# POOL's weight differences in the experts' arms: two operations of 512 columns in place of one of 1,024

## The chip, the cores and the metric

One core of a Trainium2 chip runs the whole kernel as one program. The metric is the device time of that program in microseconds, the median of the runs shown. The engines are named as the profile names them: PE multiplies matrices (PEld is its weight load), DVE is the vector engine, ACT the scalar engine, POOL is GpSimd, and SP's queue issues most of the DMAs.

## The reference

The program computes attention with a few sink keys and a sliding window, and feeds its output to a layer of eight experts in which a token may stay with the expert of the token before it.

```python
scores = scale * np.matmul(q, k.transpose(0, 1, 3, 2))      # B, H, S, D = 4, 8, 768, 64
keep = is_sink | in_window                                  # 4 sinks, window of 128
...                                                         # softmax over the kept keys
x = attn_out.transpose(0, 2, 1, 3).reshape(B, S, H * D)     # 3,072 tokens of 512
e = fresh_e if s == 0 or local_gate[b, s] < 0.5 else prev_e # one expert of 8 for each token
h = np.maximum(x[b, s] @ w1[e], 0.0)                        # 512 -> 1,024
out[b, s] = p[e] * (h @ w2[e])                              # 1,024 -> 512, times the gate
```

## The kernel before

The first part, up to about 255 us of the span, is attention, routing and the scatter of the tokens into the DRAM tensor `xs`, sorted by expert. The change does not touch it.

The second part walks over the eight experts. PE multiplies in a float32 form with shortened mantissa, so each operand is split into a high part (a rounding copy) and a low part (the difference of the original and the high part). A product is the sum of high by high, low by high and high by low. Both the tokens and the weights are split this way on the core.

**Weights.** The weights of an expert come in eight chunks of 128 x 1,024 float32, four of `w1` and four of `w2`. A chunk is loaded by SP into one of seven staging buffers (`raw`, `raw_w`), by `w_load`. `w_split` then queues its split: two copies of 512 columns by ACT (L1031, the high part `h`), and the difference (L1032, the low part `l`). Chunks alternate between two ways, `ENG = (("act", "pool"), ("act", "dve"))`: for every second chunk the difference is POOL's, for the others DVE's. High and low parts of a half of an expert's weights fill one of three buffers, `w_a`, `w_b` and `w_c`. For a `w2` chunk the staging buffer's next load, `w_load(i + AHEAD)`, is queued behind the split.

**Arms.** How many tokens an expert has is known only at run time. For each expert the program holds 25 arms, one for each count of 32-token blocks, and all engines jump to the one that is needed. In an arm, `ffn1` makes eight tiles of the hidden layer (`h`, in PSUM, three buffers; L1126, or L1115 where the group has at most seven blocks), ACT writes their high part to `hq` (L1137) and DVE their low part (L1102). `ffn2` and `second` make the second product (L1175). In between PE transposes the next expert's tokens (`xp`, L427, two PSUM buffers). For each of these ACT takes the high part (L430) and DVE the low part (L433).

**Order.** PE, ACT, DVE and SP run an arm's instructions in the order in which the code emits them. An `Agenda` holds pieces of work with a due time of the writer's own clock and emits them between the tiles of PE; `w_agenda` puts the splits there, with `lag` between the pieces of a chunk. POOL's queue holds the differences and the indirect DMAs of the results (L1157).

Of the kernel before, what the change touches and what calls it, by code (L numbers as in the profile page):

```python
# [23 lines left out]
E, DM, FF = 8, 512, 1024  # L24
# [46 lines left out]
def kernel(ctx, tc, qkd, vn, vs, w1, w2, nw, c_misc, c_ident, c_idw, c_small,  # L71
# [400 lines left out]
    def w1_of(e):  # L472
        return [t.rearrange("p (k f) -> p k f", k=KC) for t in half(e, 0)]

    def w2_of(e):
        return [lambda f, n=1, t=t: t[:, f * DM:(f + n) * DM] for t in half(e, 1)]
# [7 lines left out]
    halves = [slice(0, HP), slice(HP, FF)]  # L484
# [527 lines left out]
    def w_load(i, behind=None):  # L1012
        e, c = divmod(i, NCH)
        if e >= E:
            return
        t = raw_t[i % AHEAD]
        if c < KC:
            d = nc.sync.dma_start(t, w1[e, c * P:(c + 1) * P, :])
            if behind is not None:
                tc.add_manual_dep(d.ins, behind.ins.name, mybir.DependencyInfo(  # L1020
                    mybir.DependencyClass.Sync, mybir.DependencyReason.DATA), reason="behind the jumps")
        else:
            w2_load(t, e, c - KC)

    def w_split(ag, i, t, eng, lag=0.9):
        e, c = divmod(i, NCH)
        raw = raw_t[i % AHEAD] if e else second_raw[c - KC]
        h, l = [t[:, c, :] for t in w1_of(e)] if c < KC else [t(2 * (c - KC), 2) for t in w2_of(e)]
        hi = nc.scalar.copy if eng[0] == "act" else nc.vector.tensor_copy
        lo = (nc.gpsimd if eng[1] == "pool" else nc.vector).tensor_tensor  # L1030
        todo = [lambda s=s: hi(h[:, s], raw[:, s]) for s in halves]  # L1031
        todo += [lambda s=s: lo(out=l[:, s], in0=raw[:, s], in1=h.bitcast(F32)[:, s], op=ALU.subtract)  # L1032
                 for s in ([slice(0, FF)] if eng[1] == "pool" else halves)]
        for k, f in enumerate(todo):
            ag.add(t + lag * k, f)
        if e and c >= KC:
            ag.add(t + lag * (len(todo) - 1), lambda: w_load(i + AHEAD))

    def w_agenda(ag, e, c0, c1, t0, step, eng):
        for c in range(c0, c1):  # L1040
            w_split(ag, e * NCH + c, t0 + step * (c - c0), eng[c % len(eng)], min(0.9, 0.5 * step))
# [405 lines left out]
```

## Time and profile before

| | |
|---|---|
| time before, median of three runs | 572.18 us (572.16 to 575.89) |
| the profiled execution | 568.84 us, span 567.1 us |
| PE busy | 524.3 us, 92% of the span |
| DVE busy | 337.2 us, 59% |
| ACT busy | 283.3 us, 50% |
| POOL busy | 227.2 us, 40% |
| POOL's differences of weights in the arms (L1032) | 28 of 128x1024, 69.2 us in all (25.1 + 24.7 + 19.4) |

The span is the time from the first to the last instruction of the program in one profiled execution; that execution's own time holds 1.74 us beside it. A row of a timeline gives the start in us from the span's start, the duration in us, engine, line, operation, output and inputs, shape and count; what stands in brackets is the idle time of that engine just before, and what ended it. "issue" in that place means that the profile shows nothing that was waited for.

### The profile page before, as it was taken

The page shows a single profiled execution, that of the slowest core. Times are in us where ns is not written, and L with a number is a line of the kernel's source. Part 1 is how long each engine was busy: PE and PEld are TensorE (multiplying, and loading weights), DVE is VectorE, ACT ScalarE, POOL GpSimd, SP SyncE. Part 2 cuts the span into 40 slices and gives each one's busy share as a digit, 9 for nine tenths or more (in the row PEclk, how much of TensorE's full clock was granted, in tenths as well). Part 3 has the DMA queues.
Part 4 walks back from the last instruction along what each step waited for, and adds up shares of the span by engine and source line. Part 5 has one row for each costly group of instructions (what it writes and reads, how often), then busy time and mean ns, then how long its engine had stood idle before and what let it go on. Part 6 is the DMA issues. An engine that isn't in the chain of part 4 may idle for free. (4 is left out here: it accounts for less than half of the span.)

```text
span 567.1 us, 11850 instructions
## 1 busy us (share of the span) xinstructions
PE 524.3 (92%) x3947; PEld 446.9 (79%) x3947; DVE 337.2 (59%) x1270; ACT 283.3 (50%) x854; POOL 227.2 (40%) x191
## 2 busy tenths in 40 slices
PE   6699989979997989998999999899999999999994
PEld 3498878768886868778989788879877688889893
DVE  4677868787877878655348184753464947253321
ACT  3588867776877785253344181624332544124120
POOL 3963616383466064425350161544403544104101
PEclk8599979998998999999999999999999999999998
DMA  8634313162426025366760274737514765111000
GB/s 296 228 140 180 114 66 123 59 230 82 157 94 225 2 106 194 119 192 206 222 227 30 79 271 143 279 111 270 166 41 153 237 200 222 56 45 37 20 24 35
DMA packets 30474, 80.54 MB, mean 142 GB/s; under 512 B 3646, under 2 KB 5310, under 8 KB 30272
## 3 DMA queue, kind: packets, MB, share of 16 engines
q1 hardware_dynamic: 25520, 65.41, 33.9%
q0 software_dynamic: 4176, 12.64, 5.9%
q14 instruction: 147, 1.20, 0.7%
q8 instruction: 55, 0.90, 0.7%
q10 hardware_dynamic: 576, 0.39, 0.2%
HBM read 63.41 MB, written 16.06 MB: 140 GB/s over the span
## 5 line engine op out<-in xcount | busy, mean ns | idle before, releaser
L621 ACT ACTIVATE pef<-smf,biasf 128x264 f32<-128x264 f32 (+2 forms) x192 | 93.6, 489 | 43.2 <-DVE biasf L618 43.0
L1137 ACT ACTIVATE hq<-h 128x32 fp32r<-128x32 f32 (+4 forms) x112 | 32.0, 316 | 141.7 <-PE h L1126 92.5
L1102 DVE SCALAR_TENSOR_TENSOR hq<-h,hq 128x32 fp32r<-128x32 f32 (+4 forms) x112 | 34.4, 332 | 67.2 <-ACT hq L1137 65.6
L618 DVE CUSTOM_DVE_ANT_0 smf<-sf,mask 128x264 f32<-128x264 f32 (+2 forms) x192 | 66.6, 402 | 10.2 <-PE sf L606 9.8
L1175 PE MATMUL late<-w_a,hq 128*128 128x512 f32 (+2 forms) x288 | 70.4, 398 | 1.2 <-issue 1.2
L1175 PEld LDWEIGHTS late<-w_a,hq 128*128 128x128 f32 (+2 forms) x288 | 50.8, 179 | 16.1 <-issue 2.1
L1157 POOL DMA_INDIRECT out_dram<-ot_d,oi_d x18 | 18.9, 1051 | 92.3 <-DVE ot_d L1156 72.6
L636 PE MATMUL tpf<-ident,pef 128*128 128x128 f32 x352 | 53.4, 294 | 0.3 <-ACT ptf L643 0.2
L643 ACT COPY ptf<-tpf 128x512 f32<-128x512 f32 (+1 forms) x96 | 51.0, 531 | 1.7 <-PE tpf L636 1.6
L672 PE MATMUL avf<-ptf,v 128*64 128x128 f32 x704 | 49.8, 282 | 0.0
L636 PEld LDWEIGHTS tpf<-ident,pef 128*128 128x128 f32 x352 | 40.3, 148 | 8.2 <-ACT ptf L643 1.4
L1175 PE MATMUL late<-w_b,hq 128*128 128x512 f32 (+1 forms) x168 | 40.5, 397 | 1.8 <-issue 1.8
L672 PEld LDWEIGHTS avf<-ptf,v 128*64 128x64 f32 x704 | 38.0, 138 | 4.9 <-issue 0.3
L1175 PEld LDWEIGHTS late<-w_b,hq 128*128 128x128 f32 (+1 forms) x168 | 30.7, 184 | 9.8 <-ACT x_a L430 2.0
L578 DVE TENSOR_TENSOR xb<-bkf,rsf 128x256 f32<-128x256 f32 x48 | 20.3, 423 | 30.3 <-ACT ptsf L653 28.6
L1032 POOL TENSOR_TENSOR w_c<-raw,w_c 128x1024 fp32r<-128x1024 f32 x10 | 25.1, 2515 | 31.1 <-ACT w_c L1031 26.0
L606 PE MATMUL sf<-w_a 64*128 64x264 f32 (+2 forms) x288 | 28.6, 333 | 9.3 <-POOL w_a L136 6.2
L621 ACT ACTIVATION_READ_ACCUMULATOR pef<-smf,biasf 128x1 f32 x192 | 36.3, 189 | 0.0
L1126 PEld LDWEIGHTS h<-x_a,w_c 128*128 128x128 f32 x288 | 34.4, 188 | 0.5 <-issue 0.3
L1032 POOL TENSOR_TENSOR w_a<-raw,w_a 128x1024 fp32r<-128x1024 f32 x10 | 24.7, 2465 | 25.0 <-ACT w_a L1031 19.4
L1126 PE MATMUL h<-x_a,w_c 128*128 128x256 f32 x288 | 34.6, 281 | 0.0
L606 PEld LDWEIGHTS sf<-w_a 64*128 64x128 f32 x288 | 22.4, 216 | 14.9 <-POOL w_a L136 7.0
(225 smaller groups left out, 1089.6 us busy)
## 6 DMA issues: line engine op xcount, KB each, us to landing
raw<-in_dram SPq DMA_DIRECT2D x53, 512.0 KB, 5.3
raw<-in_dram SPq DMA_DIRECT2D x14, 800.0 KB, 6.0
xr_0n<-xs SPq DMA_DIRECT2D x21, 258.0 KB, 4.5
v<-in_dram SPq DMA_DIRECT2D x7, 768.0 KB, 4.6
raw_w<-in_dram SPq DMA_DIRECT2D x7, 512.0 KB, 4.9
raw<-in_dram SPq DMA_DIRECT2D x10, 256.0 KB, 4.6
xs<-zrow SPq DMA_DIRECT2D x9, 258.0 KB, 5.2
xr_0r<-xs SPq DMA_DIRECT2D x8, 258.0 KB, 3.0
```

Source lines behind the costliest of these rows:

```text
L578: nc.vector.tensor_tensor(out=xb[:, i, g * HG * D:(g + 1) * HG * D].rearrange("p (r t d) -> p r t d", r=NPR, t=2), in0=av[:, :, 0:P].rearr ...
L606: u["mm"] = nc.tensor.matmul(sps[:, t, :w], qx[ROWS[t], i * P:(i + 1) * P], kx[ROWS[t], off:off + w], start=m == 0, stop=m == 2)
L618: u["dve"] = nc.vector.tensor_tensor_reduce(out=sm[:, :w], in0=sps[:, t, :w], in1=mk, scale=-0.125, scalar=BIG, op0=ALU.add, op1=ALU.min, ...
L621: nc.scalar.activation(pe[:, h, :w], sm[:, :w], AF.Exp, bias=bias[:, t:t + 1], scale=-1.0, accum_out=z[:, h, 0:1])
L636: nc.tensor.transpose(tp[:, t, k, :], pe[:, 2 * c + t, o:o + P], ident)
L643: nc.scalar.copy(pt[:, :, 0:nt, :], tp[:, :, 0:nt, :])
L672: nc.tensor.matmul(avt[ROWS[t], pr, :], prep["v"][:, j, 2 * pr + t, :], x["pt"][:, t, k, :], start=i < 2 and pr == 0 and k == 0, stop=pr = ...
L1032: todo += [lambda s=s: lo(out=l[:, s], in0=raw[:, s], in1=h.bitcast(F32)[:, s], op=ALU.subtract) for s in ([slice(0, FF)] if eng[1] == "po ...
L1102: nc.vector.scalar_tensor_tensor(out=d[:, :, 1, :], in0=h, scalar=0.0, in1=d.bitcast(F32)[:, :, 0, :], op0=ALU.max, op1=ALU.subtract)
L1126: nc.tensor.matmul(hs, w[:, k, fs], x, start=t == 0, stop=t == len(mm) - 1)
L1137: relu = nc.scalar.activation(d[:, :, 0, :], h, AF.Relu)
L1175: nc.tensor.matmul(o, a, w, start=t == 0, stop=t == len(mm) - 1, skip_group_check=half)
```

## The change

In `w_split`, the difference that POOL makes was one operation over all 1,024 columns of a chunk. It becomes two operations over 512 columns each, one queued `lag` behind the other on the agenda, as DVE's were already. The copies by ACT stay two of 512 columns. Where the chunk is one of `w2`, the piece that emits the staging buffer's next load is due with the last piece of the split, and so one `lag` later on the agenda's clock.

```diff
         lo = (nc.gpsimd if eng[1] == "pool" else nc.vector).tensor_tensor
         todo = [lambda s=s: hi(h[:, s], raw[:, s]) for s in halves]
         todo += [lambda s=s: lo(out=l[:, s], in0=raw[:, s], in1=h.bitcast(F32)[:, s], op=ALU.subtract)
-                 for s in ([slice(0, FF)] if eng[1] == "pool" else halves)]
+                 for s in halves]
         for k, f in enumerate(todo):
             ag.add(t + lag * k, f)
         if e and c >= KC:
```

The sequences of PE, DVE, ACT and SP stay the same, instruction by instruction. What differs is POOL's sequence, and what some instructions of the other engines wait for.

POOL, in the arm that expert 3 takes in the profiled execution (11 blocks, 352 tokens), with what each instruction waits for. `w_b` takes the `w2` of this expert, `w_c` the `w1` of the next, and `ot` is a tile of results. Before:

```order
L1032 TENSOR_TENSOR w_b<-raw,w_b 128x1024 [waits DMAHW4_49,DMAHW1_49,DMAHW6_49,PE_49,DMAHW7_49,Activation_49,Pool_49]
L1032 TENSOR_TENSOR w_b<-raw,w_b 128x1024 [waits DMAHW0_49,DMAHW1_49,PE_49,DMAHW3_49,Activation_49,Pool_49]
L1157 DMA out_dram<-ot_10_d_40466,oi_10_d_40467 3072x512 [waits DMASW6_49,DVE_49]
L1032 TENSOR_TENSOR w_c<-raw,w_c 128x1024 [waits PE_49,DMAHW0_49,Activation_49,Pool_49]
L1032 TENSOR_TENSOR w_c<-raw,w_c 128x1024 [waits PE_49,DMAHW2_49,Activation_49,Pool_49]
L1157 DMA out_dram<-ot_10_0_2_40639,oi_10_0_2_40640 3072x512 [waits DMASW7_49,DVE_49]
```

The same place of the changed kernel:

```order
L1032 TENSOR_TENSOR w_b<-raw,w_b 128x512 [waits DMAHW4_49,DMAHW6_49,DMAHW1_49,DMAHW7_49,PE_49,Activation_49]
L1032 TENSOR_TENSOR w_b<-raw,w_b 128x512 [waits PE_49,Activation_49]
L1032 TENSOR_TENSOR w_b<-raw,w_b 128x512 [waits DMAHW1_49,DMAHW3_49,DMAHW0_49,Activation_49]
L1032 TENSOR_TENSOR w_b<-raw,w_b 128x512 [waits PE_49,Activation_49]
L1157 DMA out_dram<-ot_10_d_40734,oi_10_d_40735 3072x512 [waits DMASW6_49,DVE_49]
L1032 TENSOR_TENSOR w_c<-raw,w_c 128x512 [waits DMAHW0_49,PE_49,Activation_49]
L1032 TENSOR_TENSOR w_c<-raw,w_c 128x512 [waits PE_49,Activation_49]
L1032 TENSOR_TENSOR w_c<-raw,w_c 128x512 [waits DMAHW2_49,PE_49,Activation_49]
L1032 TENSOR_TENSOR w_c<-raw,w_c 128x512 [waits PE_49,Activation_49]
L1157 DMA out_dram<-ot_10_0_2_40910,oi_10_0_2_40911 3072x512 [waits DMASW7_49,DVE_49]
```

Four operations became eight, each with a wait of its own for ACT's copy of its half. Their waits for POOL's own earlier work are gone, and the indirect DMAs of the results keep their places between the chunks.

PE, in the same arm, at the first matrix products of `ffn2` (`o` is the tile of the last 96 tokens). Before:

```order
L1175 MATMUL o_10_0_2_40609<-w_b,hq 96x512 [waits Activation_49]
L1175 MATMUL o_10_0_2_40609<-w_b,hq 96x512
L1175 MATMUL o_10_0_2_40609<-w_b,hq 96x512 [waits Pool_49]
L1175 MATMUL o_10_0_2_40609<-w_b,hq 96x512 [waits Activation_49]
L1175 MATMUL o_10_0_2_40609<-w_b,hq 96x512 x2
L1175 MATMUL o_10_0_2_40609<-w_b,hq 96x512 [waits Activation_49]
```

And in the changed kernel:

```order
L1175 MATMUL o_10_0_2_40879<-w_b,hq 96x512 [waits Activation_49]
L1175 MATMUL o_10_0_2_40879<-w_b,hq 96x512
L1175 MATMUL o_10_0_2_40879<-w_b,hq 96x512 [waits Pool_49]
L1175 MATMUL o_10_0_2_40879<-w_b,hq 96x512 [waits Activation_49]
L1175 MATMUL o_10_0_2_40879<-w_b,hq 96x512
L1175 MATMUL o_10_0_2_40879<-w_b,hq 96x512 [waits Pool_49]
L1175 MATMUL o_10_0_2_40879<-w_b,hq 96x512 [waits Activation_49]
```

The product that reads the second half of a low part now has a wait for POOL of its own, where the one wait, three products earlier, had stood for the whole chunk. No instruction was added on PE for it.

## The prediction, made before the changed kernel ran

> **What bounds the kernel now.** I read the page's shares first, then the stretches of the second part, then PE's gaps there.
>
> ```profile
> PE 524.3 (92%) x3947; PEld 446.9 (79%) x3947; DVE 337.2 (59%) x1270; ACT 283.3 (50%) x854; POOL 227.2 (40%) x191
> 335.00:365.00 30.00, 28.31 (x154) 24.12 (x153) 19.03 (x41) 13.53 (x33) 12.93 (x7) 1.00 0.56 182
> 425.00:455.00 30.00, 28.17 (x151) 21.27 (x149) 20.12 (x49) 12.40 (x35) 12.26 (x6) 1.00 0.55 185
> sum 312.00, PE 297.16 PEld 256.48 DVE 151.97 ACT 110.50 POOL 100.65; mean PE 27.01 PEld 23.32 DVE 13.82 ACT 10.04 POOL 9.15
> ```
>
> PE sets the time. The last row sums eleven stretches from 255 us to the end: PE is busy for 297.16 of 312 us. Two of the stretches (columns: PE, PEld, DVE, ACT, POOL, granted clock, DMA share, GB/s) are those where most is lost, under 2 us each, and the granted clock there is 1.00. POOL is busy for a third of the time. So POOL's work matters only through those for whom it makes PE wait. The rows of PE's timeline that have a gap of over 0.2 us ahead of them:
>
> ```profile
> 268.78 5.85 PE L1175 MATMUL late<-w_b,hq 128*128 128x512 f32 x24 [1.78 <-issue]
> 316.15 5.85 PE L1175 MATMUL late<-w_a,hq 128*128 128x512 f32 x24 [0.96 <-issue]
> 363.18 0.63 PE L427 MATMUL xp_0n<-ident,xr_0n 128*128 128x128 f32 x4 [1.69 <-issue]
> 425.91 5.85 PE L1175 MATMUL late<-w_a,hq 128*128 128x512 f32 x24 [0.24 <-issue]
> 439.64 1.28 PE L1115 MATMUL h<-x_a,w_b 128*128 128x320 f32 x8 [0.29 <-DVE hq L1102]
> 449.42 5.83 PE L1175 MATMUL late<-w_c,hq 128*128 128x512 f32 x24 [1.01 <-issue]
> 456.50 16.89 PE L1126 MATMUL h<-x_b,w_a 128*128 128x384 f32 x96 [1.25 <-issue]
> ```
>
> They come to 7.22 us. Five of them (5.24 us) stand at the edge of an arm, ahead of the first products behind a jump or of a new arm, where the profile names no engine. The other two (1.98 us) lie inside arms, and both are DVE's, as the next rows show. That is the whole stake: 0.35% of 568.84.
>
> ```profile
> 357.27 0.62 ACT L1031 CAST w_b<-raw 128x512 fp32r<-128x512 f32 x1
> 358.26 0.64 ACT L1031 CAST w_b<-raw 128x512 fp32r<-128x512 f32 x1
> 359.03 2.40 POOL L1032 TENSOR_TENSOR w_b<-raw,w_b 128x1024 fp32r<-128x1024 f32 x1 [1.85 <-ACT w_b L1031]
> 357.93 0.68 DVE L1032 TENSOR_TENSOR w_b<-raw,w_b 128x512 fp32r<-128x512 f32 x1
> 359.37 2.61 DVE L1032 TENSOR_TENSOR w_b<-raw,w_b 128x512 fp32r<-128x512 f32 x1
> 361.90 0.57 DVE L1102 SCALAR_TENSOR_TENSOR hq<-h,hq 128x96 fp32r<-128x96 f32 x2
> 362.40 0.68 DVE L433 TENSOR_TENSOR x_b<-xp_0n,x_b 128x512 fp32r<-128x512 f32 x1
> ```
>
> The same DVE operation takes 0.68 us at 357.93 and 2.61 us at 359.37. The second runs beside POOL's difference and ends at 361.98, 0.55 us behind POOL's end at 361.43: DVE stood still until POOL was through. Then come L1102 and L433, which ends at 363.08 and gives free the PSUM buffer that PE's transposes at 363.18 need. PE's gap of 1.69 us is DVE's stall of 1.93, handed on.
>
> **The change, part by part.** First what an operation costs POOL. The rows are of two views by line (ns: least, median, greatest); the last is another loop of the kernel with the new shape.
>
> ```profile
> L1032 POOL TENSOR_TENSOR w_c<-raw,w_c x10: 2362/2398/2922, 262.3 to 476.6; 128x1024 fp32r<-128x1024 f32 x10
> L1032 POOL TENSOR_TENSOR w_a<-raw,w_a x10: 2387/2406/2826, 277.9 to 521.9; 128x1024 fp32r<-128x1024 f32 x10
> L1032 POOL TENSOR_TENSOR w_b<-raw,w_b x8: 2387/2403/2544, 287.2 to 464.7; 128x1024 fp32r<-128x1024 f32 x8
> L508 POOL TENSOR_TENSOR w_a<-raw,w_a x8: 1270/1281/1328, 201.2 to 217.9; 128x512 fp32r<-128x512 f32 x8
> ```
>
> 28 operations of 2.40 us become 56 of 1.28: two halves take 2.56, so 0.16 us more for a chunk and 28 x 0.16 = 4.5 us more POOL work. On the path this costs nothing, since POOL stands idle for two thirds of these stretches; without that cover it would be 4.5 us, 0.8%. And a chunk is done earlier. The first half need not wait for ACT's second copy: at 359.03 ACT had ended its copies at 357.89 and 358.90, about 1 us apart, so the second half could start as before and end 2.40 - 1.28 = 1.1 us sooner. Where the copies follow each other directly (0.62 apart), the end moves by 0.62 + 2.40 - 2.56 = 0.46 us. Who gains from that?
>
> ```profile
>   DVE oi_d L1151: 1.6, 1
>   PEld late L1175: 0.2, 1
> SPq L494 <- POOL w_c L1032: 7.6, 4, 2.1
> SPq L494 <- POOL w_a L1032: 7.2, 4, 2.3
> SPq L494 <- POOL w_b L1032: 1.4, 1, 1.4
> ```
>
> The first two rows are all that waited for L1032 on engines, with their total; PEld's 0.2 us was under running products. SP's loads of staging buffers (L494) wait for POOL nine times, 16.2 us in all, and would start 0.5 to 1.1 us sooner. As the load's place in SP's sequence is the same, the later due time in `w_split` costs nothing; and since PE nowhere waits for weights, an earlier load is worth nothing either. The added waits of PE and ACT for POOL sit on instructions that are there already. The new one on PE stands three products (some 1.2 us) behind the old, with the weights done well before: I take zero. For a ceiling I use the 0.05 us of a separate wait on another queue of this trace, times three such waits for each of eight experts: 1.2 us.
>
> ```profile
> L1126 PEldq EVENT_SEMAPHORE  x16: 51/51/51, 274.0 to 513.2; - x16
> ```
>
> Now the stalls. What DVE does when POOL has two operations in a row is shown at two other places.
>
> ```profile
> 17.88 1.87 POOL L136 TENSOR_TENSOR hq<-raw,hq 128x800 fp32r<-128x800 f32 x1
> 19.71 1.79 POOL L136 TENSOR_TENSOR w_a<-raw,w_a 128x544 fp32r<-128x544 f32 x1
> 18.13 2.17 DVE L136 TENSOR_TENSOR w_a<-raw,w_a 128x512 fp32r<-128x512 f32 x1 [1.40 <-ACT w_a L131]
> 202.44 1.33 POOL L508 TENSOR_TENSOR w_a<-raw,w_a 128x512 fp32r<-128x512 f32 x1
> 202.57 1.27 DVE L346 TENSOR_TENSOR exf<-exf,ohs 128x48 f32<-128x48 f32 x1
> ```
>
> At 18.13 DVE waited for POOL's first operation and ended at 20.30, 0.55 us behind that one's end and long before the end of POOL's second, which was queued right behind. So DVE, once waiting, goes first, and a stall ends with the half that runs. At 202.57 it is the new shape that blocks: DVE's operation ends 0.07 us behind POOL's.
>
> Worked out at 359: the first half is ready at about 358.0, waits for DVE's operation of 357.93 to 358.61, and runs to 359.9. DVE's next, at 359.37, waits till 359.9 and ends at 360.6 in place of 361.98. That is 1.4 us earlier, and PE's gap shrinks by about that: **1.3 us**, bounded by zero and 1.69. At 439.64 the cause is this pair:
>
> ```profile
> 435.86 2.38 POOL L1032 TENSOR_TENSOR w_c<-raw,w_c 128x1024 fp32r<-128x1024 f32 x1 [7.71 <-ACT w_c L1031]
> 437.40 1.39 DVE L1032 TENSOR_TENSOR w_c<-raw,w_c 128x512 fp32r<-128x512 f32 x1
> ```
>
> DVE loses 0.71 us to POOL's end at 438.24. With two halves the first can start near 434.9 and the second ends near 437.5, so the stall goes and with it **0.3 us** of PE's gap. The sum: 568.84 - 1.3 - 0.3 = 567.2 us for the profiled execution, 0.3% less. That execution was 3.3 us under the median of the runs shown, so for the median it is 572.18 - 1.6 = **570.6 us**. A measurement of this kernel tells about 1% from no change, and this is a third of that.
>
> The Trainium skill weighs on the step that was least certain. "SBUF — State Buffer", section "Who interferes with whom", says that DVE instructions with two SBUF inputs contend with POOL's reads, that whoever issues first gets the shared ports for its whole instruction, and that the other blocks fully. The rows at 359.37 and 18.13 agree. Read against the change, the rule would let POOL's second half go first whenever it is issued ahead of DVE's operation; the second rival prices that from rows. By the rule read so the sum would be 571.4 us, by the row at 18.13 it is 570.6.
>
> **The rivals.** *Nothing is left of the gain (0.20).* POOL's halves fall on DVE at other moments, what is won at 363 is lost elsewhere, and the time is 572.2.
>
> ```profile
> L1032 DVE TENSOR_TENSOR w_a<-raw,w_a 128x512 fp32r<-128x512 f32 x14 | 12.9, 963 | 0.0
> L1032 DVE TENSOR_TENSOR w_b<-raw,w_b 128x512 fp32r<-128x512 f32 x12 | 11.6, 977 | 0.0
> L1032 DVE TENSOR_TENSOR w_c<-raw,w_c 128x512 fp32r<-128x512 f32 x12 | 8.6, 740 | 0.0
> ```
>
> For it: against 0.68 us for an undisturbed one, these three groups (mean ns behind the busy time) lose some 8 us, and PE lost only 2 us, so most stalls fall where PE has slack, and it is chance which do not. Against it: halves stall DVE for about half as long, wherever they fall.
>
> *POOL keeps the ports through both halves (0.12).* DVE at 359.37 then waits until 361.2 at best (358.6 + 2.56) and the gain there is 0.75 us; if it arrives early in the first half, it waits 0.16 us longer than now. Time: 571.4 to 572.4. The row at 18.13 speaks against it.
>
> *New stalls in the arms, slower (0.10).* POOL's first halves start up to 1 us sooner, and so DVE meets POOL where it did not. The place that hurts is an L1032 of DVE queued ahead of L433, the low part of the next tokens: PE has two PSUM buffers for the transposes, and waits when both are held. The price is that of the place at 363, at most 1.69 us, or 1.3 with a half. Two such new places outweigh the 1.6 us; four give 572.18 - 1.6 + 5.2 = 575.8, and six would be over 1%.
>
> *The edges of the arms shift (0.05).* The five gaps ahead of jumps, 0.24 to 1.78 us, have no releaser and may hang on which transfers run then. Loads that start sooner could clear them (-5.2, 565.4) or add as much at the edges that have none (575.8 to 580).
>
> **How the numbers follow.** The forecast, a gain of 1 to 2.3 us, has 0.53; its own range is 569.9 to 571.2. The range to the other cases: below, the two gaps and one or two edge gaps gone (4 us, 568.0); above, two new stalls of 1.3 us on top of the time before (574.8, so 575.0), which takes in the ceiling of 1.2 us for the waits. Over 1% faster needs all the edge gaps and DVE's to clear together (565.4): 0.02. Over 1% slower needs six new stalls or most of the edges: 0.03.
>
> **What would show it.** 56 operations of L1032 on POOL at 1.28 us; no DVE operation beside them above about 2 us; the gap ahead of L427 in expert 3's arm under 0.5 us; the product counts and the edge gaps as now. I am wrong if DVE's longest L1032 still takes 2.6 us, if PE gets gaps inside other arms, or if the edge gaps change by more than the two that I count.

## The result, and the profile after

The changed kernel takes 577.87 us (median of 22 runs, 573.33 to 580.0) against 571.03 us for the kernel before in 22 runs beside it. The ratio is **1.0114, with a 95% interval of 1.0095 to 1.0133**: about 6.5 us slower. The forecast was 570.6 us with a range of 568.0 to 575.0. So the forecast was wrong in sign, and the time lies outside the range.

First the page's shares, and the second part of the span (window: length; then PE, PEld, DVE, ACT and POOL busy, granted clock, DMA share, GB/s).

```profile
PE 529.6 (92%) x3947; PEld 449.9 (78%) x3947; DVE 347.4 (60%) x1270; ACT 283.7 (49%) x854; POOL 235.7 (41%) x219
255.00:577.00 322.00, 302.09 (x1746) 259.39 (x1744) 162.76 (x403) 110.75 (x283) 109.92 (x87) 0.98 0.41 136
```

The same window of the kernel before:

```profile
255.00:567.10 312.10, 297.16 (x1740) 256.48 (x1738) 151.97 (x403) 110.50 (x283) 100.65 (x58) 0.99 0.41 140
```

The page's instruction counts agree but for POOL's 28 more. In this window PE's idle time grew from 14.94 to 19.91 us, by 4.97. That is the part of the loss that lies in PE's waits. DVE is busy 10.8 us longer for the same 403 operations, so it stands still for longer. PE's busy time grew as well, over the whole span by 5.3 us at the same 3,947 products, and here the granted clock is the place to look:

```profile
255.00:275.00 20.00, 18.41 (x115) 16.24 (x114) 8.65 (x34) 5.69 (x16) 9.83 (x9) 0.91 0.55 176
425.00:455.00 30.00, 26.70 (x146) 20.09 (x145) 18.06 (x59) 11.81 (x37) 9.03 (x8) 0.94 0.53 170
```

The kernel before had 1.00 in both stretches. Two later runs with the same new gaps (the changed kernel repeated, and the one with `w2` alone split) had 1.00 in both as well, so I take these two dips for the luck of this one execution. They may be why the two profiled executions lie 9.9 us apart and the medians only 6.8; no run shows that.

Now the rows of PE's timeline in the arms with a gap of over 0.2 us ahead of them, as quoted for the kernel before:

```profile
269.63 7.38 PE L1175 MATMUL late<-w_b,hq 128*128 128x512 f32 x24 [1.59 <-ACT x_a L430]
287.96 1.68 PE L1126 MATMUL h<-x_a,w_c 128*128 128x256 f32 x12 [0.79 <-DVE hq L1102]
319.72 5.86 PE L1175 MATMUL late<-w_a,hq 128*128 128x512 f32 x24 [1.03 <-issue]
337.73 0.63 PE L427 MATMUL xp_0n<-ident,xr_0n 128*128 128x128 f32 x4 [1.79 <-issue]
391.76 9.78 PE L1126 MATMUL h<-x_b,w_c 128*128 128x256 f32 x84 [1.63 <-issue]
402.54 1.68 PE L1126 MATMUL h<-x_b,w_c 128*128 128x256 f32 x12 [1.00 <-DVE hq L1102]
432.47 5.85 PE L1175 MATMUL late<-w_a,hq 128*128 128x512 f32 x24 [0.32 <-issue]
439.07 7.01 PE L1115 MATMUL h<-x_a,w_b 128*128 128x320 f32 x48 [0.76 <-PE late L1175]
450.09 1.76 PE L1115 MATMUL h<-x_a,w_b 128*128 128x320 f32 x8 [2.09 <-DVE xm L429]
464.98 16.91 PE L1126 MATMUL h<-x_b,w_a 128*128 128x384 f32 x96 [0.46 <-PE late L1175]
533.26 1.69 PE L1126 MATMUL h<-x_a,w_c 128*128 128x256 f32 x12 [0.79 <-DVE hq L1102]
```

The two gaps inside arms that the prediction wanted to shrink (1.98 us) are gone. **Five new ones** stand at other places, at 287.96, 337.73, 402.54, 450.09 and 533.26: 0.79 + 1.79 + 1.00 + 2.09 + 0.79 = 6.46 us. The gaps at the edges of arms come to 5.79 us (5.24 before). So of PE's 4.97 us more of idle time, 4.48 lie inside arms.

What stands behind the gap at 287.96 is read from POOL and DVE in expert 1's arm. POOL first:

```profile
283.43 1.00 POOL L1157 DMA_INDIRECT out_dram<-ot_d,oi_d  x1 [1.06 <-ACT hq L1137]
284.45 2.57 POOL L1032 TENSOR_TENSOR w_a<-raw,w_a 128x512 fp32r<-128x512 f32 x2
```

and DVE, from the later of its two differences on:

```profile
284.37 3.21 DVE L1032 TENSOR_TENSOR w_a<-raw,w_a 128x512 fp32r<-128x512 f32 x1
287.50 0.74 DVE L1102 SCALAR_TENSOR_TENSOR hq<-h,hq 128x256 fp32r<-128x256 f32 x2
```

POOL issues the indirect DMA and then, without a pause, both halves of a `w2` chunk, from 284.45 to 287.02. DVE's second difference begins at 284.37, 0.08 us ahead of POOL's first half, and ends at 287.58, 0.56 us behind POOL's second: 3.21 us instead of 0.68. Behind it waits L1102, which frees the `h` buffer that PE needs. The same place before:

```profile
280.95 1.00 POOL L1157 DMA_INDIRECT out_dram<-ot_d,oi_d  x1 [0.69 <-PE h L1126]
282.94 2.39 POOL L1032 TENSOR_TENSOR w_a<-raw,w_a 128x1024 fp32r<-128x1024 f32 x1 [0.98 <-ACT w_a L1031]
281.29 1.28 DVE L1032 TENSOR_TENSOR w_a<-raw,w_a 128x512 fp32r<-128x512 f32 x2
```

There POOL waited 0.98 us more for ACT's second copy, and DVE got both of its differences done in that time, at full speed. This is what the split took away: the first half needs only ACT's first copy.

Three more operations of DVE in the arms are as long. They stand ahead of the gaps at 402.54, 450.09 and 533.26.

```profile
398.91 3.25 DVE L1032 TENSOR_TENSOR w_a<-raw,w_a 128x512 fp32r<-128x512 f32 x1
445.88 3.37 DVE L1032 TENSOR_TENSOR w_c<-raw,w_c 128x512 fp32r<-128x512 f32 x1
529.66 3.20 DVE L1032 TENSOR_TENSOR w_a<-raw,w_a 128x512 fp32r<-128x512 f32 x1
```

The fifth gap, at 337.73 in expert 2's arm, is of another kind. There the indirect DMA stands between the two halves, and one half was enough:

```profile
333.44 1.27 POOL L1157 DMA_INDIRECT out_dram<-ot_d,oi_d  x1 [0.15 <-PE h L1126]
334.72 1.32 POOL L1032 TENSOR_TENSOR w_c<-raw,w_c 128x512 fp32r<-128x512 f32 x1
334.31 2.29 DVE L1032 TENSOR_TENSOR w_c<-raw,w_c 128x512 fp32r<-128x512 f32 x1
```

DVE's operation lies ahead of an L433 that frees a PSUM buffer of the transposes, and PE waits for that.

Not every meeting of the two goes like this. Later in expert 2's arm POOL's first half began 0.10 us ahead of DVE:

```profile
343.18 1.31 POOL L1032 TENSOR_TENSOR w_a<-raw,w_a 128x512 fp32r<-128x512 f32 x1 [0.81 <-ACT w_a L1031]
344.44 1.75 POOL L1032 TENSOR_TENSOR w_a<-raw,w_a 128x512 fp32r<-128x512 f32 x1
343.28 1.76 DVE L1032 TENSOR_TENSOR w_a<-raw,w_a 128x512 fp32r<-128x512 f32 x1
```

Here DVE was done at 345.04, 0.55 us behind the first half, and it was POOL's second half that took 1.75 us. DVE came in between, as the prediction had it.

It is not enough to ask who began first. In expert 3's arm DVE began 0.05 us ahead of POOL's first half (0.08 in expert 1's) and ran at full speed (ACT's copy for that half, DVE, then POOL's two halves):

```profile
362.67 0.62 ACT L1031 CAST w_b<-raw 128x512 fp32r<-128x512 f32 x1
363.32 0.68 DVE L1032 TENSOR_TENSOR w_b<-raw,w_b 128x512 fp32r<-128x512 f32 x1
363.37 3.49 POOL L1032 TENSOR_TENSOR w_b<-raw,w_b 128x512 fp32r<-128x512 f32 x2 [1.21 <-ACT w_b L1031]
```

The copy that POOL's half needed ended at 363.29, 0.03 us before DVE began. In expert 1's arm the copy for POOL's half is this one:

```profile
283.29 0.61 ACT L1031 CAST w_a<-raw 128x512 fp32r<-128x512 f32 x1
```

It ended at 283.90, so that POOL's half had stood ready for 0.47 us when DVE began, with only POOL's own indirect DMA still ahead of it. In the changed kernel this parts the cases without exception. In five, DVE began first but behind such a ready operation, and it was kept out (the four long ones and the one at 334.31). In eight, DVE began first and POOL's operation became ready at most 0.03 us before that, or later, and DVE took 0.68 us.

### The profile page after: what moved, and what is told of

Read it like the earlier page. It is cut to its first block, busy times and chain, and to the rows that moved or that the text cites. A ratio compares the mean times of both kernels' runs of the same rounds, so it can differ in the third digit from the quotient of the medians.

```text
span 577.0 us, 11888 instructions
## 1 busy us (share of the span) xinstructions
PE 529.6 (92%) x3947; PEld 449.9 (78%) x3947; DVE 347.4 (60%) x1270; ACT 283.7 (49%) x854; POOL 235.7 (41%) x219
## 5 line engine op out<-in xcount | busy, mean ns | idle before, releaser
L1102 DVE SCALAR_TENSOR_TENSOR hq<-h,hq 128x32 fp32r<-128x32 f32 (+4 forms) x112 | 34.0, 331 | 67.1 <-ACT hq L1137 65.6
L1175 PEld LDWEIGHTS late<-w_a,hq 128*128 128x128 f32 (+2 forms) x288 | 50.7, 179 | 16.2 <-issue 2.3
L1175 PE MATMUL late<-w_b,hq 128*128 128x512 f32 (+1 forms) x168 | 42.0, 408 | 1.6 <-ACT x_a L430 1.6
L1175 PEld LDWEIGHTS late<-w_b,hq 128*128 128x128 f32 (+1 forms) x168 | 31.9, 191 | 10.0 <-ACT x_a L430 1.8
L1032 POOL TENSOR_TENSOR w_c<-raw,w_c 128x512 fp32r<-128x512 f32 x20 | 27.6, 1399 | 25.8 <-ACT w_c L1031 25.7
L1032 POOL TENSOR_TENSOR w_a<-raw,w_a 128x512 fp32r<-128x512 f32 x20 | 26.8, 1365 | 27.4 <-ACT w_a L1031 27.3
L562 PE MATMUL bkf<-idw,xtf 128*128 128x146 f32 x192 | 33.8, 300 | 0.4
```

Of the source, the lines that this page charges most:

```text
L562: mm = nc.tensor.matmul(bk[:, pr * WX:(pr + 1) * WX], blk["xt"][:, pr, :], idw[:, g * NPR + pr, :], start=True, stop=True, skip_group_chec ...
L1102: nc.vector.scalar_tensor_tensor(out=d[:, :, 1, :], in0=h, scalar=0.0, in1=d.bitcast(F32)[:, :, 0, :], op0=ALU.max, op1=ALU.subtract)
L1175: nc.tensor.matmul(o, a, w, start=t == 0, stop=t == len(mm) - 1, skip_group_check=half)
```

## The experiments

My theory after this result: in the `w2` chunks at the start of an arm POOL starts about 1 us sooner, right behind the indirect DMA; DVE's second difference meets it there and is kept out through **both** halves, since nothing stands between them. The rivals: a single half is enough for the loss; two halves without a pause keep DVE out wherever they meet it; the loss comes from the `w1` chunks; the new waits of PE and ACT, or the clock, are behind it. The edits below are against the changed kernel unless said otherwise. A "long stall" is an operation of DVE's beside POOL's that took 2.5 us or more beyond its 0.68; the changed kernel has four. A ratio below is against the kernel before, run beside that kernel; the level differs between these sets (medians of the kernel before of 573.09, 572.66 and 584.08 us), so the times in the expectations, which count from about 571, are best read as ratios.

**Which chunks?** Two kernels split POOL's operation in one kind of chunk alone.

```diff
-                 for s in halves]
+                 for s in ([slice(0, FF)] if eng[1] == "pool" and c < KC else halves)]     # w2 alone is split
...
+                 for s in ([slice(0, FF)] if eng[1] == "pool" and c >= KC else halves)]    # w1 alone is split
```

> Two operations for the chunks of w2 alone (14 of 28); those of w1 stay one of 1,024. The long stalls of DVE in the changed kernel (3.2 to 3.4 us at 284, 399, 446 and 530 us) all stand in the first tiles of an arm, where w2 is split. Early-start theory: nearly all of the loss is here, 575 to 578. Two-holds theory: the loss follows the count of pairs, half of it, 573 to 575.

> The other half: two operations for the chunks of w1 alone (14 of 28), one for those of w2. Early-start theory: little of the loss, 570 to 572.5. Two-holds theory: half of it, 573 to 575.

With only the `w2` chunks split the ratio is 1.0123 [1.0068, 1.0178] and all four long stalls are there, with PE's gaps at the same five places (0.79, 1.79, 0.80, 2.08 and 0.79 us).

With only the `w1` chunks split it is 0.9993 [0.9948, 1.0038], without a long stall, and the old gap ahead of L427 in expert 3's arm is back at 1.64 us. So the loss comes from the `w2` chunks, all of it as near as the intervals tell, and so does the gain that was forecast in expert 3's arm. Of the second kernel's profile only the stalls and that gap are used: its execution took 577.37 us, against a median of 573.21.

**Start later, by order.** The halves in the other order, so that the first to run needs ACT's second copy.

```diff
-                 for s in halves]
+                 for s in (halves[::-1] if eng[1] == "pool" else halves)]
```

> POOL still makes two operations of 512 columns, but takes the second half first, so that it starts when ACT's second copy is done, as the one operation did. Early-start theory (the first half begins up to 1 us sooner than before and lands on DVE's pair of differences, which then stands for both halves): the start is back where it was, DVE's stalls of over 2 us go, PE's gaps inside arms fall from about 7 us to under 3, and the time is 570 to 572.5, about 1% under the changed kernel. Two-holds theory (two operations with no wait between them keep DVE out whatever their start): stalls of 2.5 us stay and the time is 576 to 579.

This tested nothing of the kind. POOL's instructions came out in their old order, the first half first: in expert 1's arm POOL's pair began at 282.98, before ACT's second copy ended at 283.59. So it repeats the changed kernel: 1.0082 [1.0041, 1.0124], four long stalls, in-arm gaps of 1.03, 1.77, 1.02, 2.08 and 0.77 us. It is of use as a second measurement. Its in-arm gaps are 4.69 us above those of the kernel before, 0.8% of 571, which is all of its ratio.

**Start later, by a dependency.** The first half waits for ACT's second copy as well.

```diff
+            if eng[1] == "pool" and len(lows2) == 1:
+                tc.add_manual_dep(lows2[-1].ins, copies[1].ins.name, ..., reason="both copies first")
```

> Two operations of 512 columns, the first of which also waits for ACT's second copy, so that POOL starts where it started before the change; the second half of a w2 chunk then waits for the completion of the first, as in e2. If the loss is DVE being kept out through both halves where it arrives ahead of POOL's first: in expert 1's arm POOL starts its second w2 chunk 8.4 us after the arm's first product (7.4 in the changed kernel), DVE's pair is through by 8.1, none of the four stalls of 2.5 us is left and the time is 569 to 572.5, ratio 0.995 to 1.002. If the loss is the longer work of POOL or the number of its operations, both are still there and the time stays above 575.

The ratio is 0.9985 [0.995, 1.0021]. No operation of DVE's stalls by more than 1.12 us. Expert 1's arm:

```profile
287.40 1.00 POOL L1167 DMA_INDIRECT out_dram<-ot_d,oi_d  x1 [0.56 <-DVE ot_d L1166]
289.38 2.54 POOL L1037 TENSOR_TENSOR w_a<-raw,w_a 128x512 fp32r<-128x512 f32 x2 [0.98 <-ACT w_a L1034]
287.74 1.28 DVE L1037 TENSOR_TENSOR w_a<-raw,w_a 128x512 fp32r<-128x512 f32 x2
```

These are the rows of the kernel before, with two halves in place of one operation: POOL's 0.98 us of waiting is back, and DVE's pair runs in it. The pause that was expected in the `w2` chunks is not there: in all 28 chunks POOL's second half begins 0.03 to 0.05 us before the first ends, as it mostly does in the changed kernel, where the next kernel has at least 0.08 us between them. So this kernel changes the start alone. It keeps the two halves and, with them, PE's separate waits for each, so neither the number of operations nor those waits make the loss.

**Only a pause.** POOL starts as early as in the changed kernel, but the second half waits until the first is complete.

```diff
+            if eng[1] == "pool" and len(half) == 2:
+                tc.add_manual_dep(half[1].ins, half[0].ins.name, ..., reason="a pause between the halves")
```

> The changed kernel, with POOL's second half waiting for the completion of its first (a semaphore of POOL on itself, as the operations of 1,024 columns had ahead of them before the change). Two-holds theory: DVE gets in between the halves, no stall of DVE beside L1032 is over 1.5 us, and the time falls by half or more of the loss, to 571 to 574.5. Early-start theory: the collisions stay, each costs 1.3 in place of 2.5 us, and the time falls by at most a third of the loss, to 575 to 577.5.

The ratio is 1.0026 [0.9991, 1.0062]. At the four places the stalls are now 1.27, 1.28, 1.47 and 1.28 us, and none anywhere is over 1.6 (1.60 at the fifth place, a little over the 1.5 expected). Expert 1's arm again, POOL's pair and DVE's operation:

```profile
287.56 3.02 POOL L1035 TENSOR_TENSOR w_a<-raw,w_a 128x512 fp32r<-128x512 f32 x2
287.48 1.95 DVE L1035 TENSOR_TENSOR w_a<-raw,w_a 128x512 fp32r<-128x512 f32 x1
```

DVE begins 0.08 us ahead of POOL as in the changed kernel, to the hundredth, but its stall is 1.27 us: it ends at 289.43, 0.56 us behind the first half (which ran from 287.56 to 288.87), and it is POOL's second half, from 288.95 on, that takes longer. So the early start alone doesn't make the long stall, and by the kernel above two operations with no wait between don't make it alone either; it takes both. PE's gaps of 1.00 and 0.79 us behind such stalls are gone and 2.09 became 0.87, while 1.78 at the fifth place stays, where the DMA stood between the halves anyway.

```profile
340.35 0.63 PE L427 MATMUL xp_0n<-ident,xr_0n 128*128 128x128 f32 x4 [1.78 <-issue]
448.81 1.28 PE L1122 MATMUL h<-x_a,w_b 128*128 128x320 f32 x8 [0.87 <-DVE xm L429]
```

**Move the meeting.** The store that queues the indirect DMA is due earlier on the agenda's clock, and nothing else is changed.

```diff
-                    ag.add(2.5 * time1(ng) / FC, lambda: store_late(0, nm))
+                    ag.add(1.5 * time1(ng) / FC, lambda: store_late(0, nm))
```

> The changed kernel, with the store of the late tile (its DVE part and its indirect DMA on POOL) due one tile of ffn1 earlier in an arm, so that POOL's indirect DMA is over before DVE's pair of w2 differences begins. If what counts is who comes first: POOL's first half begins ahead of DVE's second operation there, DVE gets in between the halves, its stalls there fall from 2.5 to 1.1 us or less, and the time falls to 571 to 575. If DVE is kept out through both halves whatever comes first: stalls of 2.5 us stay and the time stays at 576 to 579.

The ratio is 0.9989 [0.9953, 1.0026], with one long stall left (2.60 us, PE's gap 1.92 at 446.68). Expert 1's arm:

```profile
284.98 1.00 POOL L1157 DMA_INDIRECT out_dram<-ot_d,oi_d  x1 [0.15 <-DMA raw<-in_dram]
286.50 1.57 POOL L1032 TENSOR_TENSOR w_a<-raw,w_a 128x512 fp32r<-128x512 f32 x1 [0.52 <-PE h L1126]
286.83 1.80 DVE L1032 TENSOR_TENSOR w_a<-raw,w_a 128x512 fp32r<-128x512 f32 x1
288.04 1.74 POOL L1032 TENSOR_TENSOR w_a<-raw,w_a 128x512 fp32r<-128x512 f32 x1
```

The DMA is done early, POOL's first half stands idle for 0.52 us behind it and now begins 0.33 us ahead of DVE's second operation, and DVE is let in between the halves (1.80 us), though they are still queued back to back. So the operations and their sizes are those of the changed kernel; only the moment of the meeting has moved, and no loss is left that the interval tells from zero.

To see whether the earlier store is worth something by itself, it was also put into the kernel before, and into the kernel of the dependency on the second copy.

> The kernel before the change (one operation of 1,024 columns), with the store of the late tile one tile earlier as in e6. It says what that edit is worth by itself. If e6 recovered because DVE no longer comes ahead of POOL's first half: here the edit is worth nothing, ratio 0.995 to 1.003. If the earlier store is a gain of its own that hid the loss of the two operations in e6: ratio 0.985 to 0.992.

> e5 (first half waits for both copies) with the earlier store of e6, as the version that might beat both kernels. No stall of DVE over 1.3 us, PE's gaps inside arms under 1 us, which is 1 to 2 us less than in the kernel before: ratio 0.994 to 1.000. If the rest of the gaps is at the edges of arms, it can't be told from 1.

The first gives 0.9965 [0.9927, 1.0003], not told from no change, and not the 0.985 to 0.992 that it would have to be if the earlier store had merely covered up an unrelated loss of the halves. It may still be worth something: PE's old gap of 1.69 us in expert 3's arm is gone there, which is 0.3%, while the changed kernel with the earlier store, at 0.9989, still has 1.92 us of gaps inside arms. The second, with halves, late start and earlier store, gives 0.9956 [0.9918, 0.9995], and no stall is over 1.13 us. Its ratio is the lowest of all, by an interval that just excludes no change, but it isn't told from the 0.9965 of the earlier store alone.

**Four operations.** If DVE is kept out for as long as POOL has operations queued, quarters should stall it for the length of four.

```diff
-                 for s in halves]
+                 for s in (quarters if eng[1] == "pool" else halves)]      # four of 256 columns
```

> Four operations of 256 columns for each chunk of POOL, with no wait between the first and second and between the third and fourth but for data. About 0.72 us each (0.73 to 0.74 for the 256 columns of another loop), 2.9 us for a chunk. If DVE that arrives first is kept out by all that is queued on POOL: stalls of 2.7 to 3 us where the changed kernel has 2.5, and 577 to 581. If it is kept out by two operations, whatever their size: stalls of about 1.3 us there, and 571 to 575.

In expert 1's arm (POOL's DMA, its four quarters as one row, and DVE's operation):

```profile
281.72 1.00 POOL L1158 DMA_INDIRECT out_dram<-ot_d,oi_d  x1 [0.16 <-issue]
282.74 2.82 POOL L1033 TENSOR_TENSOR w_a<-raw,w_a 128x256 fp32r<-128x256 f32 x4
282.37 3.75 DVE L1033 TENSOR_TENSOR w_a<-raw,w_a 128x512 fp32r<-128x512 f32 x1
```

DVE ended at 286.12, 0.56 us behind the fourth quarter. At three of the four places DVE was kept out through all four (stalls of 2.79 to 3.07 us); at the fourth place it got in after 0.2 us, though POOL's first quarter had stood ready for 0.69 us. The part of the expectation on stalls held at those three, the part on time did not: the ratio is 0.999 [0.9952, 1.0027]. With the quarters the two dearest places, of 1.79 and 2.09 us in the changed kernel, happened to be free, and the three left cost 1.38, 1.07 and 1.05 us. A stall costs time only where PE has no slack: in the kernel before, DVE's at 469.13 is 2.21 us long, and PE has no gap behind it.

The in-arm gaps (over 0.2 us) and the ratios side by side:

| kernel | PE's gaps inside arms, us | long stalls | ratio [95%] |
|---|---|---|---|
| before | 1.98 | 0 | 1 |
| before, earlier store | 0.30 | 0 | 0.9965 [0.9927, 1.0003] |
| start with second copy | 0.91 | 0 | 0.9985 [0.995, 1.0021] |
| changed, earlier store | 1.92 | 1 | 0.9989 [0.9953, 1.0026] |
| only a pause | 2.65 | 0 | 1.0026 [0.9991, 1.0062] |
| four operations | 3.50 | 3 | 0.999 [0.9952, 1.0027] |
| only `w2` split | 6.25 | 4 | 1.0123 [1.0068, 1.0178] |
| changed | 6.46 | 4 | 1.0114 [1.0095, 1.0133] |
| changed, repeated | 6.67 | 4 | 1.0082 [1.0041, 1.0124] |

The three kernels above 6 us are the three that are measurably slower.

## Why the prediction was wrong, point by point

**What bounds the kernel, and where the stake lies: right.** PE bounds it still, and the loss is where the text looked for the gain, in DVE's stalls handed on to PE inside arms.

**What an operation costs: right, but it was not all.** By line the halves are as forecast (ns: least, median, greatest):

```profile
L1032 POOL TENSOR_TENSOR w_c<-raw,w_c x20: 1276/1291/1795, 262.0 to 485.7; 128x512 fp32r<-128x512 f32 x20
...
L1032 POOL TENSOR_TENSOR w_b<-raw,w_b x16: 1282/1342/1782, 288.2 to 474.4; 128x512 fp32r<-128x512 f32 x16
```

POOL's busy time grew by 8.5 us (227.2 to 235.7), not 4.5: the rest is halves that were held up by DVE and took up to 1.8 us each. No wait of PE names POOL's L1032.

**Added waits at zero: right.** In the view of waits no row has PE waiting for POOL's L1032. The three products between the old wait and the new are 0.73 us by the rows (24 take 5.85), not 1.2; nothing hung on it.

**Loads that start earlier are worth nothing: nothing speaks against it.** SP's waits for POOL's differences fell from 16.2 to 7.6 us (2.6 + 2.5 + 2.5, rows below), and no gain is to be seen.

```profile
SPq L494 <- POOL w_b L1032: 2.6, 3, 1.2
SPq L494 <- POOL w_a L1032: 2.5, 2, 1.3
SPq L494 <- POOL w_c L1032: 2.5, 2, 1.2
```

**The gain of 1.3 + 0.3 us at the two places: right.** Both gaps went, 1.98 us in all. In expert 3's arm DVE's difference took 0.93 us in place of 2.61, and PE's transposes follow without a gap in PE's timeline:

```profile
364.76 0.93 DVE L1032 TENSOR_TENSOR w_b<-raw,w_b 128x512 fp32r<-128x512 f32 x1
366.90 0.63 PE L427 MATMUL xp_0n<-ident,xr_0n 128*128 128x128 f32 x4
```

The gap at 439.64 is gone as well, though the same arm got the new one of 2.09 us one tile of `h` later.

**The step that failed** is "DVE, once waiting, goes first, and a stall ends with the half that runs". It was generalised from two rows, at 18.13 and 202.57, in both of which DVE arrived after POOL's first operation had begun. Counted over the changed kernel and five of the kernels above (the repeat, `w2` alone, `w1` alone, the start with the second copy, the earlier store), that case holds without exception: 50 of 50 got in between the halves, with stalls of at most 1.14 us. What failed is the case in which POOL's operation stood ready behind POOL's own indirect DMA before DVE began. In the same six kernels the copy that POOL needed (copies and operations paired by their order) had then ended 0.19 to 0.83 us before DVE's start, and DVE, though it began 0.07 to 0.41 us ahead of POOL, was kept out in 16 of 16: through both halves in the 13 where the second followed at once (stalls of 2.52 to 2.77 us), through the one half in the other three (1.6 us). Where that copy ended at most 0.06 us before DVE began, or later, DVE began first as well and ran undisturbed in 53 of 53. So DVE does not always go first once it waits, and a stall can last through every half that is queued. Before the change this could not be seen: POOL's operation was one, and it waited for ACT's second copy, and mostly for POOL's own earlier work (the `Pool_49` in its order, gone in the changed kernel).

A second fault made the first one dear. The sum re-timed the stalls that were there and did not ask where POOL's earlier start would make new ones. The rival *new stalls in the arms* named it ("POOL's first halves start up to 1 us sooner") but got a chance of 0.10, a price of 1.3 us "with a half", and a high end of the range from two new places. The runs showed five, at 0.79 to 2.09 us, so 6.46 us less the 1.98 that went. A table of DVE's differences in all arms against ACT's first copies, instead of at the two places with a gap, would have shown expert 1's arm (DVE's pair at 281.29 in POOL's wait that ended at 282.94) as one about to collide. The rival *POOL keeps the ports through both halves* had the mechanism and applied it only to the one old place, where it did not occur.

The rule that the prediction weighed, of "SBUF — State Buffer", section "Who interferes with whom", in the Trainium skill, has whoever issues first hold the shared ports for its whole instruction. The rows at 343.18 and 343.28 agree with it. By the profile's start times the rows at 284.37 and 284.45 don't: DVE was first, and it lost. They agree if POOL's half counts as issued from 283.90, when the copy it needed was done; that is a reading of the counts above, and no row shows the moment at which an operation asks for the ports. Why DVE stayed out through the second half too, the rule doesn't say.

**What stays open.** Why a DVE operation that meets a ready half is kept out through the next one as well, while one that comes after the first half's start gets in between, was not settled; that a pause between the halves ends it was. That readiness decides was read by sorting the meetings; the later start and the earlier store both remove it and the long stalls with it (one is left with the earlier store, where the half was ready 0.19 us before DVE began), but the fourth place with four operations goes against it. And the gaps inside arms explain 4.5 us of the 6.5. Those at edges come to 0.55 more, but the repeat of the same kernel has 7.31 us there in place of 5.79, so that is within their own variation. The repeat, at 1.0082, needs no more than the gaps inside arms, while the interval of 1.0095 to 1.0133 leaves 0.4 to 2.6 us beyond all gaps unexplained.

## What to carry to other kernels

When an operation of an engine off the critical path is cut up, its first piece waits for less and starts sooner: list what it will run beside *then*, in every place of the loop, before counting what gets shorter. A wait that costs its own engine nothing may be what keeps it out of another's way; here POOL's 0.98 us of idling for a copy was DVE's undisturbed time. And a rule for contention taken from two rows holds for the order in those rows only; ask for each operation not only when it begins but from when it stood ready.

## What was not expected of the hardware

- A DVE difference that begins while POOL's operation already stands ready behind POOL's indirect DMA is not served until every half queued without a wait between is through, though by the profile DVE begins first: 13 of 13, 3.20 to 3.37 us in the changed kernel in place of 0.68. With four operations of 256 columns it waited for all four at three places of four.
- One that begins first where POOL's operation is not yet ready, or has just become so, runs undisturbed: 53 of 53.
- One that starts after POOL's first has begun is served between them: 50 of 50, and then POOL's second is the one that is held up (1.75 us in place of 1.28 at 344.44).
- A wait of POOL for its own previous operation, though only 0.08 us passes between the two, is enough to let DVE in: the stall at the same place fell from 2.5 to 1.27 us.
